# Attention and two expert layers on one core: a key copy to ScalarE, three multiplications to VectorE, one weight piece behind two query loads

## The chip, the cores and the metric

The kernel runs on one core of one Trainium2 chip. The metric is the device time of one execution in microseconds. A core has five engines with a stream of instructions each: PE (TensorE, matmuls, with PEld for its weight loads), DVE (VectorE), ACT (ScalarE), POOL (GpSimd) and SP (SyncE, which only issues DMAs here). An engine works through its stream in order, and waits on semaphores for the others and for DMAs.

## The reference

Inputs are q, k, v (2 batches, 8 heads, 768 positions, 64 columns) and the weights of two dense layers. Attention of a query goes to the keys within 16 positions and to 24 block keys (the maximum over each block of 32); the layers follow on 1536 tokens of width 512.

```python
k_sum = k.reshape(B, H, nb, block, D).max(axis=3)
v_sum = v.reshape(B, H, nb, block, D).mean(axis=3)
scores_s = scale * einsum('bhsd,bhnd->bhsn', q, k_sum) + log(block)
a = softmax(concat([where(|i - j| < 16, scale * q @ k.T, -1e9), scores_s]))
x = a @ concat([v, v_sum])
h = x @ w_in;   x = (h * sigmoid(1.702 * h)) @ w_out          # 512 -> 2048 -> 512
x = (sigmoid(x @ w_gate) * (x @ w_val)) @ w_out2              # 512 -> 1536 -> 512
```

## The kernel before, in words

Attention is cut into 24 units: batch (2) by group of four blocks of 64 queries (3) by pair of heads (4). Unit u of batch 0 uses the keys k0_(u mod 4); units 0 to 3 are group 0, units 12 to 23 are batch 1. For each unit `w_copy` (L693) makes a scaled copy kx of the keys that its four blocks see: 96 windowed columns a block (128x384) and 32 block keys a block (128x128), on POOL. `b_pe` (L706) computes mask and scores into PSUM (ps_s, L710 and L712), `b_max` (L715) their maximum on DVE, `b_exp` (L720) the exponentials on ACT, with the sums beside them, `n_inv` (L730) the reciprocal sums on DVE, and `n_mul` (L737) multiplies the 128x512 exponentials e by them, on POOL. `c_pe` (L741) transposes e on PE (ps_p, L745), `c_copy` (L748) copies that from PSUM (ACT for the first ten units), `d_pe` (L753) multiplies by the values vwin and the block values vs (ps_x, L764), `d_hi` (L781) and `d_lo` (L784) write the result as high and low part, xH on ACT and xL on DVE.

The units are written out as a software pipeline: in step t the part with lag n works on unit t - n. The list is

```python
ORDER = [
    (w_copy, -1), (b_pe, 0), (b_max, 0), (n_inv, LN), (n_mul, LN),
    (c_pe, LC), (c_copy, LC), (d_pe, LD), (d_hi, LD), (b_exp, 0), (d_lo, LD),
]
```

with LN = 1 and LC = LD = 3. From step 8 on, pieces of the first expert layer are put between the units (a generator, `filler`): hidden products ps_h, a sigmoid on ACT (L524), its product with the hidden value on DVE (L500), a cast of the result into gh on ACT (L508) and its rest gl, and the output products ps_o (L489). Sigmoid and exponential are different table sets of ACT; a load (ACT_TABLE_LOAD) stands in its stream wherever it goes from one to the other. Every product is made of three, because each fp32 operand is split into a high and a low part.

After attention come the rest of layer 1 (eight groups of hidden columns) and layer 2 (six groups), in which PE runs without a hole.

Loads are issued by SP in the order in which the program writes them. `load_q` (L632, 256 KB a unit, five buffers) runs five units ahead, `load_k` (L626) brings 400 KB a head pair, `load_v` (L642) 768 KB a group, `put_v` (L650) lays the block values of 256 KB beside them, the first time through ACT's queue. `fetch` (L229) issues the next megabyte of weights from a list: first group 0's w_in (`raw1_0_0`), then group 0's w_out, whose name is 1_0_1 and which goes into a buffer with the tag xH, then group 1's. In step 0, `fetch` is called behind the loads of the second group's values, and the load of q6 stands in step 1.

SP's stream is the order of the program. The order of PE, DVE, ACT and POOL is set by the framework's scheduler, which lists the instructions by its own estimate of when each can start; where durations or dependencies change, the order changes with them.

Of the kernel before, what the change touches and what calls it, by code (L numbers as in the profile page):

```python
# [13 lines left out]
AF = mybir.ActivationFunctionType  # L14
ALU = mybir.AluOpType
AX = mybir.AxisListType
PSUM = bass.MemoryType.PSUM
P = 128
# [11 lines left out]
def attention_moe_moe2_kernel(ctx: ExitStack, tc: tile.TileContext, ins: dict, out: bass.AP):  # L30
    nc = tc.nc
# [4 lines left out]
    B, HP, _, S = vt.shape  # L36
# [8 lines left out]
    G = 4  # L45
# [7 lines left out]
    scale = 1.0 / float(D) ** 0.5  # L53
# [169 lines left out]
    for layer, g, i in wanted:  # L223
        w = mats[layer][i]
        last = i == len(mats[layer]) - 1
        x = w.bitcast(U32)
        pieces.append((f"{layer}_{g}_{i}", rows_of(x, g) if last else cols_of(x, g, 2)))

    def fetch():  # L229

        if pieces:
            name, src = pieces.pop(0)
            n, m = src.shape[1], src.shape[2]

            home, tag = (xp, "xH") if name == "1_0_1" else (wraw, "raw")
            raw = home.tile([P, n * m], U32, tag=tag, name=f"{tag}{name}")
            nc.sync.dma_start(out=raw.rearrange("p (a n) -> p a n", a=n), in_=src)
            raws.append((raw, (P, n, m // 2)))
# [357 lines left out]
    def pull(n):  # L596
        for _ in range(n):
            next(coming, None)
# [9 lines left out]
    with tc.manual_schedule(engines={mybir.EngineType.SP}), ExitStack() as es:  # L608
# [17 lines left out]
        def load_k(b, hp):  # L626

            t = kp.tile([P, SH], F32, tag="k", name=f"k{b}_{hp}")
            nc.sync.dma_start(out=t, in_=k[b, hp])
            kraw[b, hp] = t  # L630

        def load_q(u, eng):  # L632

            b, g, hp = units[u]
            t = qp.tile([P, G, P], F32, tag="q", name=f"q{u}")
            eng.dma_start(out=t.rearrange("p i c -> p (i c)"), in_=q[b, g, hp])
            qbd[u] = t
# [4 lines left out]
        def load_v(b, g):  # L642
            c = (b * NG + g) % 2 * G
            first_row = v[b, g * G * QB:g * G * QB + P - W0, :]
            src = bass.AP(
                first_row.tensor, first_row.offset, [first_row.ap[0], [QB * H * D, G], [1, H * D]]
            )
            nc.sync.dma_start(out=vwin[W0:P, c:c + G, :], in_=src)

        def put_v(b, g, eng=nc.sync):  # L650
            c = (b * NG + g) % 2 * G
            src = vsum[b][0:W0].unsqueeze(1).to_broadcast([W0, G, H * D])
            eng.dma_start(out=vwin[0:W0, c:c + G, :], in_=src)
# [5 lines left out]
        def sum_load(b, hp):  # L659
            if (b, hp) == (0, 2):  # L660
                early = xp.tile([P, 2, KC * TB // 2], F32, tag="xL", name="vt_early")
                vtl["early"] = [early[:, i, 0:S] for i in range(2)]
            if b == 0 and hp > 1:
                t = vtl["early"][hp - 2]
            else:
                t = vp.tile([P, S], F32, tag="vt", bufs=2, name=f"vt{b}_{hp}")
            nc.sync.dma_start(out=t, in_=vt[b, hp])
            vtl[b, hp] = t

        def sum_v(b, hp):  # L670
            if hp == 0:
                vpart[b] = vp.tile([P, HP, W0], F32, tag="vm", name=f"vm{b}")
                nc.vector.memset(vpart[b], 0.0)
            nc.vector.tensor_reduce(
                out=vpart[b][:, hp, 0:NB], in_=vtl.pop((b, hp)).rearrange("p (n t) -> p n t", t=BLK),
                axis=AX.X, op=ALU.add,
            )

        def sum_lay(b):
            r = vpart.pop(b)  # L680
            ps = ps_a.tile([W0, H * D], F32, tag="x", name="ps_v", bufs=2)
            for hp in range(HP):
                nc.tensor.matmul(ps[:, hp * P:(hp + 1) * P], lhsT=r[:, hp], rhs=ident, start=True, stop=True)
            nc.scalar.activation(vsum[b][0:W0], ps, AF.Copy, scale=1.0 / BLK)

        def prep_k(b, hp):
            ks = kp.tile([P, W0], F32, tag="ks", name=f"ks{b}_{hp}")
            nc.vector.memset(ks, 0.0)
            own = kraw[b, hp][:, HALO:HALO + S].rearrange("p (n t) -> p n t", t=BLK)
            nc.vector.tensor_reduce(out=ks[:, 0:NB], in_=own, axis=AX.X, op=ALU.max)  # L690
            kmax[b, hp] = ks

        def w_copy(u):  # L693

            b, g, hp = units[u]
            t = kxp.tile([P, G, P], F32, tag="kx", name=f"kx{u}")
            r = kraw[b, hp][:, g * G * QB:g * G * QB + P - W0]
            src = bass.AP(r.tensor, r.offset, [r.ap[0], [QB, G], [1, P - W0]])
            top = kmax[b, hp].unsqueeze(1).to_broadcast([P, G, W0])
            for to, x in ((t[:, :, W0:P], src), (t[:, :, 0:W0], top)):  # L700
                nc.gpsimd.tensor_scalar(out=to, in0=x, scalar1=scale, scalar2=None, op0=ALU.mult)  # L701
            kx[u] = t

# [32 lines left out]

        def n_mul(u):  # L737
            e, rr = live["e", u], live.pop(("rr", u))
            nc.gpsimd.tensor_tensor(out=e, in0=e, in1=rr.unsqueeze(2).to_broadcast([P, G, P]), op=ALU.mult)

        def c_pe(u):  # L741
            e = live.pop(("e", u))
# [41 lines left out]
        def d_lo(u):  # L784
# [5 lines left out]
        LN, LC, LD = 1, 3, 3  # L790
# [4 lines that stand above are left out]
# [6 lines left out]
        for _ in range(4):  # L801
# [28 lines left out]
            out=win, in_=win, pattern=[[0, NSLOT], [1, P - W0]], compare_op=ALU.is_gt, fill=NEG,  # L830
# [3 lines left out]
            out=win, in_=win, pattern=[[0, NSLOT], [-1, P - W0]], compare_op=ALU.is_gt, fill=NEG,  # L834
# [21 lines left out]
        for t in range(-1, NU + LD):  # L856
            now[0] = t

            u = t + 2
            if u < NU and units[u][1] == 0:  # L860
                prep_k(units[u][0], units[u][2])
            for part, lag in ORDER:
                if 0 <= t - lag < NU:
                    part(t - lag)
            if 0 <= t < NU - 5:
                load_q(t + 5, nc.sync)
            if t == -1:
                sum_v(0, 0)
                sum_v(0, 1)
            if t == 0:  # L870
                sum_v(0, 2)
                sum_v(0, 3)
                sum_lay(0)
                load_v(0, 1)
                put_v(0, 1, nc.scalar)
                fetch()
            if t in (5, 8):
                fetch()
            if t in (7, 8, 9, 10):
                sum_load(1, t - 7)  # L880
            if t in (8, 9, 10, 11):
                sum_v(1, t - 8)
            if t == 11:
                sum_lay(1)

            if t % HP == HP - 1 and HP < t < NU - HP:
                c = t // HP + 1
                load_v(c // NG, c % NG)
                put_v(c // NG, c % NG)
            if 8 <= t < 8 + HP:  # L890
                load_k(1, t - 8)
            if t >= 1:
                pull(1 if t < 6 or t > 9 else 2)
            for _ in range(2 if t >= 8 else 1):
                next(fill, None)
# [164 lines left out]
```

## Time and profile before

| | before |
|---|---|
| three runs, us | 615.36, 615.39, 616.43 (median 615.39) |
| the profiled execution, us | 616.76 |
| its span, us | 615.0 |
| its mean granted clock of TensorE | 0.994 |
| instructions | 8762 |

The rows that follow below come from the profiled execution, with times in microseconds from the start of its span. The span is from the first to the last instruction; the 1.76 us between it and the execution's time lie around it.

### The profile page before, as it was taken

What the parts mean: (1) busy time and instruction counts of PE and PEld (TensorE: products, weight loads), DVE (VectorE), ACT (ScalarE), POOL (GpSimd) and SP (SyncE); (2) the same over time, 40 slices, a digit from 0 to 9 for tenths busy, and PEclk for the clock granted to TensorE, in tenths of its full rate; (3) what the DMA queues carried; (4) which work ended last, traced back from release to release, by engine and by line L of the source; (5) the groups of instructions that cost most, each with busy time, mean ns of one, the idle gap of its engine ahead of it and who ended that gap; (6) DMA issues with size and microseconds to landing.
All of it is one profiled execution on the core that took longest, in us unless ns stands there. A gap on an engine that the chain in (4) does not pass through costs nothing.

```text
span 615.0 us, 8762 instructions
## 1 busy us (share of the span) xinstructions
PE 600.4 (98%) x3342; PEld 500.6 (81%) x3342; DVE 447.2 (73%) x668; ACT 316.5 (51%) x624; POOL 188.0 (31%) x158
## 2 busy tenths in 40 slices
PE   7698999999999999999999999999999999999997
PEld 4587788788888888888888888898898898898896
DVE  6599775498998757777559889568759669777434
ACT  4779566666464535535435667635445246344230
POOL 5887586300142413313322021022022022122030
PEclk9989999999999999999999999999999999999999
DMA  9999653003142302321002023322222212200014
GB/s 307 340 277 340 225 147 69 2 10 129 48 148 78 102 36 79 115 81 58 12 1 69 0 68 100 107 69 70 68 69 69 68 69 70 69 1 0 1 51 154
DMA packets 25161, 58.10 MB, mean 94 GB/s; under 512 B 1568, under 2 KB 1824, under 8 KB 25120
## 3 DMA queue, kind: packets, MB, share of 16 engines
q1 hardware_dynamic: 24400, 56.24, 28.0%
q10 hardware_dynamic: 720, 1.31, 0.6%
q8 instruction: 26, 0.43, 0.3%
q14 instruction: 15, 0.12, 0.1%
HBM read 53.08 MB, written 3.15 MB: 91 GB/s over the span
## 4 chain that ended last, share of the span: by engine, by line
PE 93%; DMA 4%; ACT 1%; DVE 1%; POOL 0%; issue 0%; SPq 0%; POOLq 0%
PE ps_o L489 37%; PE ps_y L197 16%; PE ps_x L197 11%; PE ps_v L197 11%; PE ps_h L489 6%; PE ps_h L197 4%; PE ps_s L712 3%; DMA q<-in_q 3%; PE ps_x L764 2%; PE ps_p L745 2%; DMA k<-in_k 1%; PE ps_s L710 0%; ACT L524 0%; ACT e L725 0%; POOL kx L701 0%
## 5 line engine op out<-in xcount | busy, mean ns | idle before, releaser
L511 POOL TENSOR_TENSOR gl<-sg,gh 128x512 fp32r<-128x512 f32 x78 | 114.0, 1467 | 388.6 <-ACT gh L508 246.3
L577 DVE TENSOR_TENSOR acc<-ps_o,acc 128x512 f32<-128x512 f32 x143 | 96.6, 685 | 58.0 <-PE ps_o L489 57.7
L489 PE MATMUL ps_o<-gl,w_1H 128*128 128x512 f32 x192 | 75.4, 394 | 0.0
L489 PE MATMUL ps_o<-gh,w_1H 128*128 128x512 f32 x192 | 74.7, 390 | 0.0
L489 PE MATMUL ps_o<-gh,w_1L 128*128 128x512 f32 x192 | 71.9, 398 | 1.7 <-ACT gh L508 1.7
L508 ACT CAST gh<-sg 128x512 fp32r<-128x512 f32 x84 | 51.6, 621 | 32.8 <-DVE sg L500 24.9
L489 PE MATMUL ps_o<-w_2L,gh 128*128 128x512 f32 (+1 forms) x146 | 56.6, 387 | 0.0
L489 PE MATMUL ps_o<-w_2H,gh 128*128 128x512 f32 (+1 forms) x146 | 56.4, 386 | 0.0
L489 PE MATMUL ps_o<-w_2H,gl 128*128 128x512 f32 (+1 forms) x146 | 56.2, 389 | 0.1
L150 DVE SCALAR_TENSOR_TENSOR da<-da,db 128x1024 uint32<-128x1024 uint32 x34 | 45.7, 1343 | 8.8 <-ACT da L140 8.2
L489 PEld LDWEIGHTS ps_o<-gh,w_1L 128*128 128x128 f32 x192 | 36.1, 189 | 9.2 <-ACT gh L508 1.9
L140 ACT ACTIVATE da<-da 128x1024 f32<-128x1024 f32 x34 | 36.1, 1061 | 13.9 <-DVE da L132 10.7
L489 PEld LDWEIGHTS ps_o<-gl,w_1H 128*128 128x128 f32 x192 | 36.2, 189 | 7.3 <-issue 0.2
L489 PEld LDWEIGHTS ps_o<-gh,w_1H 128*128 128x128 f32 x192 | 36.2, 188 | 7.3
L701 POOL TENSOR_SCALAR kx<-k 128x384 f32<-128x384 f32 x24 | 33.5, 1396 | 18.2 <-PE ps_s L712 10.3
L725 ACT ACTIVATE e<-ps_s,nm 128x128 f32<-128x128 f32 x96 | 34.2, 376 | 9.3 <-DVE nm L717 7.1
L712 PE MATMUL ps_s<-kx,q 128*128 128x128 f32 x192 | 30.9, 314 | 3.3 <-DMA q<-in_q 2.4
L712 PEld LDWEIGHTS ps_s<-kx,q 128*128 128x128 f32 x192 | 28.2, 222 | 6.4 <-DMA q<-in_q 2.3
L489 PEld LDWEIGHTS ps_o<-w_2H,gh 128*128 128x128 f32 x146 | 27.4, 188 | 5.7
L489 PEld LDWEIGHTS ps_o<-w_2H,gl 128*128 128x128 f32 x146 | 27.4, 188 | 5.2 <-DVE acc L577 0.3
L489 PEld LDWEIGHTS ps_o<-w_2L,gh 128*128 128x128 f32 x146 | 27.5, 188 | 5.0
L132 DVE TENSOR_SCALAR db<-raw 128x1024 uint32<-128x1024 uint32 x33 | 28.1, 850 | 0.4
(245 smaller groups left out, 1495.7 us busy)
## 6 DMA issues: line engine op xcount, KB each, us to landing
raw<-in_moe_w_out SPq DMA_DIRECT2D x13, 1024.0 KB, 5.0
raw<-in_moe_w_in SPq DMA_DIRECT2D x8, 1024.0 KB, 7.3
raw<-in_moe_w_gate SPq DMA_DIRECT2D x6, 1024.0 KB, 5.1
raw<-in_moe_w_val SPq DMA_DIRECT2D x6, 1024.0 KB, 5.0
q<-in_q SPq DMA_DIRECT2D x20, 256.0 KB, 9.0
vwin<-in_v SPq DMA_DIRECT2D x6, 768.0 KB, 7.9
k<-in_k SPq DMA_DIRECT2D x8, 400.0 KB, 8.1
out<-acc SPq DMA_DIRECT2D x11, 256.0 KB, 2.0
```

The source lines that it names most:

```text
L132: ins = nc.vector.tensor_scalar(**x)
L140: nc.scalar.activation(af, af, AF.Prelu, scale=REBIAS, alpha=-2.0 ** 32)
L150: ins = nc.vector.scalar_tensor_tensor(out=a, in0=a, scalar=3, in1=b, op0=ALU.logical_shift_left, op1=ALU.bitwise_or)
L197: nc.tensor.matmul(ps, lhsT=a[x][:, kk, :], rhs=b[y][:, kk, :], start=start and i == 0, stop=i == n - 1, skip_group_check=True,)
L489: nc.tensor.matmul(ps, lhsT=a, rhs=b, start=i == 0, stop=i == n - 1)
L508: nc.scalar.copy(gh, sg)
L511: engine.tensor_tensor(out=gl, in0=sg, in1=gh, op=ALU.subtract)
L577: added[layer, g, blk, m] = nc.vector.tensor_tensor(out=a[:, m, :], in0=ps, in1=a[:, m, :], op=ALU.add)
L701: nc.gpsimd.tensor_scalar(out=to, in0=x, scalar1=scale, scalar2=None, op0=ALU.mult)
L712: nc.tensor.matmul(ps[:, j, :], lhsT=t[:, j, :], rhs=kt[:, j, :], start=False, stop=j == G - 1)
L725: nc.scalar.activation(e[:, j, :], s[:, j, :], AF.Exp, bias=nm[:, j:j + 1], accum_out=sm[:, j:j + 1])
L745: nc.tensor.transpose(ps[:, j, :], e[:, j, :], ident)
```

## The change

Three edits. Unit 3's two key copies (u == HP - 1, HP being 4) go by ScalarE's activation with the scale instead of POOL. The multiplication of the exponentials by their reciprocal sums goes by VectorE for units 0 to 2. And the call that fetches group 0's output weights moves from step 0 to step 2, in which it stands behind the loads of q6 and q7.

```diff
@@ w_copy
             for to, x in ((t[:, :, W0:P], src), (t[:, :, 0:W0], top)):
+                if u == HP - 1:
+                    nc.scalar.activation(to, x, AF.Copy, scale=scale)
+                    continue
                 nc.gpsimd.tensor_scalar(out=to, in0=x, scalar1=scale, scalar2=None, op0=ALU.mult)
@@ n_mul
-            nc.gpsimd.tensor_tensor(out=e, in0=e, in1=rr.unsqueeze(2).to_broadcast([P, G, P]), op=ALU.mult)
+            (nc.vector if u < HP - 1 else nc.gpsimd).tensor_tensor(out=e, in0=e, in1=rr.unsqueeze(2).to_broadcast([P, G, P]), op=ALU.mult)
@@ the steps
                 put_v(0, 1, nc.scalar)
-                fetch()
-            if t in (5, 8):
+            if t in (2, 5, 8):
                 fetch()
```

Three lines more stand ahead of what follows, so a line of the kernel before has a number higher by 3 in the changed one from L701 on, and by 2 behind the steps.

SP's queue, at the place of the moved fetch. A row is the line, the kind of instruction, and what goes into what, with the buffers' numbers. Before:

```order
L237 DMA raw1_0_0_152<-in_moe_w_in 128x4x512
L636 DMA q5_209<-in_q 128x512
L648 DMA vwin_109<-in_v 96x4x512
L237 DMA xH1_0_1_221<-in_moe_w_out 128x2x1024
L636 DMA q6_248<-in_q 128x512
L636 DMA q7_278<-in_q 128x512
L636 DMA q8_331<-in_q 128x512
```

And of the change:

```order
L237 DMA raw1_0_0_152<-in_moe_w_in 128x4x512
L636 DMA q5_209<-in_q 128x512
L648 DMA vwin_109<-in_v 96x4x512
L636 DMA q6_246<-in_q 128x512
L636 DMA q7_276<-in_q 128x512
L237 DMA xH1_0_1_278<-in_moe_w_out 128x2x1024
L636 DMA q8_331<-in_q 128x512
```

The megabyte of weights has gone behind q6 and q7; ahead of q8 stands the same as before.

PE, from the transposes of unit 4 to the scores of unit 8 (ps_p are transposes, ps_s scores and their masks, ps_x the products with the values). Before:

```order
L745 MATMUL ps_p_454<-ident_67,e_325 128x128 x4
...
L712 MATMUL ps_s_441<-kx6_386,q6_248 128x128 x4
L712 MATMUL ps_s_498<-kx7_438,q7_278 128x128 x4
L710 LDWEIGHTS pick_111
L710 MATMUL ps_s_547<-mask_110,pick_111 128x512
...
L745 MATMUL ps_p_511<-ident_67,e_377 128x128 x4
L712 MATMUL ps_s_547<-kx8_495,q8_331 128x128 x4
```

And of the change:

```order
L748 MATMUL ps_p_454<-ident_67,e_325 128x128 x4
L715 MATMUL ps_s_441<-kx6_386,q6_246 128x128 x4
L767 MATMUL ps_x_409<-pt_407,vwin_109 64x64
...
L715 MATMUL ps_s_498<-kx7_438,q7_276 128x128 x4
L748 MATMUL ps_p_511<-ident_67,e_377 128x128 x4
L713 LDWEIGHTS pick_111
L713 MATMUL ps_s_547<-mask_110,pick_111 128x512
L715 MATMUL ps_s_547<-kx8_495,q8_331 128x128 x4
```

Unit 6's scores now stand ahead of the value products, and unit 7's behind them; unit 8's scores close the piece in both.

ScalarE, around the second step's two sigmoids (sg, from the hidden products ps_h) and the exponentials e of units 14 and 15. Before:

```order
L782 CAST xH1_765<-ps_x_956 128x256
L725 ACTIVATE e_967,sm_966<-ps_s_936,nm_942 128x128 x4
L573 COPY acc1_0_853<-ps_o_918 128x512
L573 COPY acc1_0_853<-ps_o_926 128x512
L524 ACT_TABLE_LOAD
L524 ACTIVATE sg_1049<-ps_h_978 128x512
L508 CAST gh1_1_0_0_1054<-sg_1049 128x512
L524 ACTIVATE sg_1051<-ps_h_991 128x512
L508 CAST gh1_1_0_1_1059<-sg_1051 128x512
L782 CAST xH1_765<-ps_x_1027 128x256
L725 ACT_TABLE_LOAD
L725 ACTIVATE e_1038,sm_1037<-ps_s_1007,nm_1013 128x128 x4
```

And of the change:

```order
L524 ACT_TABLE_LOAD
L524 ACTIVATE sg_1049<-ps_h_978 128x512
L508 CAST gh1_1_0_0_1054<-sg_1049 128x512
L785 CAST xH1_765<-ps_x_956 128x256
L728 ACT_TABLE_LOAD
L728 ACTIVATE e_967,sm_966<-ps_s_936,nm_942 128x128 x4
L524 ACT_TABLE_LOAD
L524 ACTIVATE sg_1051<-ps_h_991 128x512
L508 CAST gh1_1_0_1_1059<-sg_1051 128x512
L785 CAST xH1_765<-ps_x_1027 128x256
L785 CAST xH1_765<-ps_x_1086 128x256
L728 ACT_TABLE_LOAD
```

The exponentials e_967 have come between the two sigmoids, with a table load on either side.

## Rows read from the trace of the kernel before

**Rows 1.** The page, busy time, share of the span and instructions of each engine.
```profile
PE 600.4 (98%) x3342; PEld 500.6 (81%) x3342; DVE 447.2 (73%) x668; ACT 316.5 (51%) x624; POOL 188.0 (31%) x158
```

**Rows 2.** Windows: start:end, length, busy us (instructions) by engine, PE clock, DMA share, GB/s.
```profile
15.00:30.00 15.00, 10.60 (x143) 8.18 (x143) 8.65 (x20) 11.13 (x42) 13.30 (x14) 1.00 1.05 337
30.00:45.00 15.00, 14.02 (x132) 11.99 (x132) 13.81 (x29) 10.36 (x38) 11.96 (x11) 0.89 0.92 273
45.00:60.00 15.00, 13.22 (x127) 10.28 (x126) 14.07 (x24) 13.94 (x39) 11.19 (x11) 0.95 1.04 372
75.00:500.00 425.00, 424.98 (x2211) 355.32 (x2210) 319.88 (x445) 224.02 (x392) 110.84 (x85) 1.00 0.22 72
```

**Rows 3.** The chain of waits in order of time: start us, us, what.
```profile
15.92 14.98 DMA q<-in_q
```

**Rows 4.** DMA issues at 11.2 (vwin), 13.1, 15.9 and 19.55: KB, us to landing.
```profile
vwin<-in_v SPq DMA_DIRECT2D x1, 768.0 KB, 14.2
xH<-in_moe_w_out SPq DMA_DIRECT2D x1, 1024.0 KB, 17.3
q<-in_q SPq DMA_DIRECT2D x1, 256.0 KB, 15.0
q<-in_q SPq DMA_DIRECT2D x1, 256.0 KB, 12.7
```

**Rows 5.** PE's timeline: start, us, line, operation, [idle before <-releaser]; units 6+7, 8, 12.
```profile
30.95 3.63 PE L712 MATMUL ps_s<-kx,q 128*128 128x128 f32 x16 [2.19 <-DMA q<-in_q]
...
36.40 1.06 PE L712 MATMUL ps_s<-kx,q 128*128 128x128 f32 x8
...
53.90 1.05 PE L712 MATMUL ps_s<-kx,q 128*128 128x128 f32 x8
...
58.21 0.61 PE L489 MATMUL ps_o<-gh,w_1L 128*128 128x512 f32 x1 [1.72 <-ACT gh L508]
```

**Rows 6.** POOL's timeline: unit 3's key copy, and unit 12's.
```profile
13.27 1.17 POOL L701 TENSOR_SCALAR kx<-k 128x384 f32<-128x384 f32 x1 [1.41 <-DMA k<-in_k]
...
49.55 1.39 POOL L701 TENSOR_SCALAR kx<-k 128x384 f32<-128x384 f32 x1 [1.37 <-DMA k<-in_k]
```

**Rows 7.** The page's groups: VectorE's accumulation; busy us, mean ns, idle before it.
```profile
L577 DVE TENSOR_TENSOR acc<-ps_o,acc 128x512 f32<-128x512 f32 x143 | 96.6, 685 | 58.0 <-PE ps_o L489 57.7
```

**Rows 8.** VectorE's timeline, its two long waits between 16 and 21 us.
```profile
16.62 0.95 DVE L674 TENSOR_REDUCE vm<-vt_early 128x24 f32<-128x768 f32 x1 [0.93 <-DMA vt_early<-in_vt]
...
20.46 1.29 DVE L717 TENSOR_REDUCE nm<-ps_s 128x4 f32<-128x512 f32 x2 [1.82 <-PE ps_s L712]
```

**Rows 9.** ScalarE's timeline: unit 1's exponentials, table loads, casts and a sigmoid's wait.
```profile
12.87 0.37 ACT L725 ACTIVATE e<-ps_s,nm 128x128 f32<-128x128 f32 x1 [1.32 <-DVE nm L717]
...
58.17 1.28 ACT L725 ACT_TABLE_LOAD   x1
59.47 0.37 ACT L725 ACTIVATE e<-ps_s,nm 128x128 f32<-128x128 f32 x1
...
60.85 0.63 ACT L508 CAST gh<-sg 128x512 fp32r<-128x512 f32 x1
...
73.78 1.28 ACT L524 ACT_TABLE_LOAD   x1 [2.85 <-PE ps_h L489]
...
76.43 0.62 ACT L508 CAST gh<-sg 128x512 fp32r<-128x512 f32 x1 [0.76 <-DVE sg L500]
```

**Rows 10.** Windows as in rows 2: the two falls of the clock, and between them 3 us.
```profile
31.50:33.00 1.50, 1.50 (x9) 1.50 (x9) 1.50 (x4) 0.00 (x0) 0.00 (x0) 0.50 1.05 382
34.50:37.50 3.00, 3.00 (x47) 2.44 (x45) 2.88 (x6) 2.33 (x12) 3.00 (x3) 0.99 0.56 171
58.50:60.00 1.50, 1.50 (x8) 1.40 (x8) 1.50 (x2) 1.49 (x4) 1.20 (x2) 0.50 1.03 233
```

## The prediction, made before the changed kernel had run

> **What bounds the kernel now.** I read the page first: TensorE is busy 98% of the span, the others 73, 51 and 31% [rows 1]. Its time can therefore only change through its few holes or its clock, and the windows say where these are: PE is busy 10.60 of 15 us from 15 to 30, and 424.98 of 425 us from 75 to 500 [rows 2]. Attention's first half is the only place where this change can win anything, and what it wins there comes off the end, because PE then has no hole left to swallow it.
>
> Next the chain of waits: one transfer of queries, from 15.92 for 14.98 us, is its longest piece, and the scores of units 6 and 7 begin when it lands [rows 3, 5]. The queue view shows why the transfer takes so long: group 0's output weights (1024 KB) are issued at 13.1 and q6 behind them at 15.9. They land 17.3 and 15.0 us later, at 30.4 and 30.9, and q8, issued at 19.55, lands 12.7 us later, at 32.25 [rows 4]. These are not slow transfers: the DMA engines are busy throughout (share 1.05) and move 337 GB/s from 15 to 30 [rows 2]. It is a backlog, in which a transfer's place decides its landing and its issue time does not.
>
> PE's own timeline then gives the dates that matter: units 6 and 7 at 30.95 after a hole of 2.19 us, unit 8 at 36.40, unit 12 at 53.90, and the first output product at 58.21 after a hole of 1.72 us behind ScalarE's cast [rows 5].
>
> **The change part by part.** *Early copies and multiplications.* POOL loses unit 3's key copy, 1.17 us and a smaller one [rows 6], and three multiplications. VectorE gains the three. None of this form ran on it; its nearest row of 128x512 elements is the accumulation at 685 ns [rows 7], so 3 x 0.685 = 2.06 us. They fall where VectorE waits: 0.93 us for a value transfer and 1.82 us for scores [rows 8], 2.75 us together. ScalarE gains two copies. Its cast of 512 columns takes 0.63 us [rows 9], so I put at most that for 384 columns and as much for 128. Unit 3's keys are there only when POOL starts on them at 13.27 after waiting 1.41 us [rows 6], and in the new order ScalarE does the first of these copies ahead of unit 1's exponentials, which began at 12.87 [rows 9]: they move to 13.27 + 0.63 = 13.90, about 1 us later. Whether this group gains or loses that microsecond, its successors wait for queries until past 30 us, so I cost it at nothing. If the queries came early enough, unit 1's delay would be the price: the bounds are 1 us lost, and 1.70 us gained (POOL's copies).
>
> *The queries' place.* Between the values issued at 11.2, which land 14.2 us later at 25.4 [rows 4], and q6 the megabyte of weights no longer stands. Then 256 KB at 337 GB/s take 0.8 us: q6 lands at about 26.2 and q7 at 27.0; with ScalarE's 256 KB value-sum transfer sharing the engines in that stretch it may be a microsecond more. Unit 6 no longer waits. But q8 and all behind it have the same bytes ahead as before and keep 32.25. In the new order PE does units 6 and 7 and the older products, comes to unit 8's scores, and waits there for q8. So unit 8 goes from 36.40 to 32.25: **4.15 us is the ceiling**, not the 30.95 - 26.2 that the move of q6 suggests. PE's work between is 36.40 - 30.95 = 5.45 us and fits behind 27.0.
>
> *What of the lead reaches the end.* From 36.40 to 45 PE has hardly a hole (14.02 us of 30 to 45 are busy, and most of the rest is the end of the hole at 30.95 [rows 2, 5]), so the lead lasts that long. Unit 12 needs the second batch's keys, for which POOL waited 1.37 us at 49.55 [rows 6]. They can come earlier only as far as the DMA engines have room. From 34.5 to 37.5 they moved 171 GB/s against 382 from 31.5 to 33.0 [rows 10]: 3 x (382 - 171) = 633 KB are missing there, which is 1.7 us at that rate. The first output product at 58.21 hangs on ScalarE, which is busy 13.94 of the 15 us from 45 to 60 [rows 2] and can start only as early as its inputs. So the lead there lies between 1.7 and 4.15. I take 2.5 us, nearer the keys, because those are the row with a wait in it.
>
> *Table loads.* The new order of ScalarE has two more table loads, as unit 14's exponentials now stand between the two sigmoids of the second step. Each costs 1.28 us [rows 9]. In that stretch ScalarE idled 2.85 us ahead of the sigmoid at 73.78 and 0.76 us ahead of its cast at 76.43 [rows 9]. The second sigmoid now comes behind load, exponentials (59.47 to 60.85 for unit 12's four, 1.38 us) and load, 1.28 + 1.38 + 1.28 = 3.94 us. Less 2.85 us that leaves 1.09, less 0.76 us as well 0.33. I take 0.6 us lost; the bounds are 0, since PE may have other work there, and the whole 3.94.
>
> *The clock.* Two stretches ran at half clock (granted 0.50, 1.2 of 2.4 GHz): one around 31.5 to 33.0, behind the 2.19 us hole, and one around 58.5 to 60.0, behind the 1.72 us hole [rows 5, 10]. Unit 6's and 7's sixteen score matmuls took 3.63 us there, unit 8's eight 1.06 us at full clock [rows 5]: 3.63 - 2 x 1.06 = 1.5 us is what the first cost at least. The first is inside the 4.15 already: its loss only delayed unit 8, which the new date of q8 replaces. If the hole ahead of unit 8 is as deep, the fall moves there and costs up to 1.5 us of the lead. The second stays if its hole stays: I take 0, with the same 1.5 us of gain as the other bound.
>
> *Sum:* 0 - 2.5 + 0.6 + 0 = **-1.9 us**. The profiled execution took 616.76 us (span 615.0), 1.37 us over the median of 615.39. Taken from the median: **613.5 us**.
>
> **The rivals.** *A, the whole lead arrives:* unit 12's keys had slack, and 4.15 us reach the end, or the second fall of the clock goes as well. For it: POOL has the first part of the copy done at 49.55 + 1.39 = 50.94, while the scores that need it come at 53.90 [rows 5, 6]. Against it: the copy waited for them at all. 615.39 - 4.15 = 611.2; with the second clock fall gone and 0.6 lost to the tables 610.3.
>
> *B, the lead is eaten:* keys and ScalarE's row of work stand where they stood, and by 58.21 nothing is left but the hole ahead of that product, now longer. For it: ScalarE has 1.06 us of slack in those 15 us, and it is its cast that ended PE's hole at 58.21 [rows 2, 5]. The same comes out if the queue does not serve in the order of issue and q6 is early in the program only. Time: 615.39 with 0.6 for the tables, 615.0 to 616.
>
> *C, slower:* PE stalls for the second sigmoid. The price is the whole 3.94 us on PE's path, against a lead of 2.5: +1.4, so 616.8. It decides from the point at which PE has no other product ready while ScalarE loads. For it: from 75 on PE has no hole that could swallow a wait [rows 2], and its order is fixed. Against it: ScalarE had its 2.85 us of idle time precisely there. The rule that would make this dearer is in the Trainium skill, "ScalarE: Activation LUTs", section "What ACT_TABLE_LOAD costs": a switch costs the load and a drain of about the same length, some 2.66 us together. By that two more would be an estimated 5.3 us. The trace differs: the load at 58.17 took 1.28 us and the exponential behind it began at 59.47, 1.30 us after the load's start [rows 9], so the measured price holds here.
>
> **How the numbers follow.** A measurement of this kernel can tell 0.2%, or 1.2 us, from no change. Forecast (611.9 to 614.4): 0.40. A: 0.17, since a wait for keys stands in the rows. B: 0.24, since ScalarE is nearly full where the lead has to pass. C: 0.19, since ScalarE's idle covers most of its price. Faster: 0.40 + 0.17 = 0.57; the same 0.24; slower 0.19. The range reaches from between the two times of A, at 610.8, to just over C, 617.0. The forecast's own range is 611.9 (a lead of 4.15 with no clock gain and 0.6 for the tables) to 614.4 (a lead of 1.7 and 0.7 lost).
>
> **What would show it.** Right: q6 lands before 28 and q8 still near 32; PE's hole of 2.19 us is ahead of unit 8 and no longer ahead of unit 6; unit 8 starts near 32.3; the first output product starts 1.7 to 4 us ahead of 58.21; between two sigmoids of the second step stand two table loads, and PE's wait behind them is under 1 us. Wrong: unit 8 starts later than 34; or the first output product is at 58 still, which is B; or PE has a hole of more than 1 us between 70 and 80, which is C. A median under 610.8 would mean that both clock falls are gone and the keys never mattered.

## The result, and the profile after

The changed kernel took **618.50 us** (median of 7 executions, 617.04 to 619.65) against 615.36 for the kernel before (7 executions, 614.20 to 616.43): slower by half a per cent, ratio 1.0052, 95% interval 1.0041 to 1.0062. Forecast were 613.5 and a range up to 617.0: the prediction was wrong in sign and in range. The profiled execution of the changed kernel took 617.66, with a span of 615.9.

The page of the changed kernel, its line of busy times, which answers to [rows 1]:

```profile
PE 600.7 (98%) x3341; PEld 500.2 (81%) x3342; DVE 451.1 (73%) x671; ACT 319.7 (52%) x628; POOL 184.4 (30%) x153
```

Its windows, with the columns of [rows 2], show where PE's holes went. From 15 to 30 it is now busy 13.76 us, against 10.60. From 70 on, where it had none, there are holes: 2.52 us between 70 and 90 and half a microsecond between 90 and 110.

```profile
15.00:30.00 15.00, 13.76 (x197) 11.40 (x195) 13.05 (x26) 12.81 (x51) 13.25 (x13) 1.00 1.05 337
45.00:60.00 15.00, 13.47 (x96) 10.00 (x91) 15.00 (x23) 10.11 (x27) 12.00 (x10) 0.89 1.00 343
70.00:90.00 20.00, 17.48 (x131) 13.76 (x133) 12.41 (x26) 13.11 (x43) 13.88 (x15) 1.00 0.86 260
90.00:110.00 20.00, 19.51 (x174) 15.86 (x175) 11.40 (x25) 13.01 (x48) 14.23 (x15) 1.00 0.28 67
```

The queue did what the forecast said. SP's timeline has q6 issued at 12.37 and q8 at 17.36:

```profile
12.37 3.59 SPq L636 DMA_DIRECT2D q<-in_q  x2
...
17.36 2.81 SPq L636 DMA_DIRECT2D q<-in_q  x2
```

and the DMA issues at 12.4 and at 17.4 show q6 landing 13.0 us later at 25.4 (30.9 before [rows 4]) and q8 14.0 later at 31.4 (32.25 before):

```profile
q<-in_q SPq DMA_DIRECT2D x1, 256.0 KB, 13.0
q<-in_q SPq DMA_DIRECT2D x1, 256.0 KB, 14.0
```

PE's timeline: unit 6 follows q6 at 25.40, unit 8 waits for q8 until 31.46, as forecast, with a hole of only 1.10 us and no fall of the clock behind it. At 52.41 PE waits for ScalarE's copy of a transpose, and at 56.05 it starts the first output product (58.21 before). The last four rows are the 2.52 us between 70 and 90: a wait for a score buffer that unit 14's exponentials give back (74.96), one for VectorE's copy of a transpose (76.02), one for the second step's second gated value (sg, multiplied by VectorE right behind ScalarE's sigmoid, 77.60), and one for a score buffer that unit 15's exponentials give back (85.16). Only 0.30 us of them is a wait for the second sigmoid.

```profile
25.40 1.16 PE L715 MATMUL ps_s<-kx,q 128*128 128x128 f32 x8 [0.25 <-DMA q<-in_q]
...
31.46 1.13 PE L715 MATMUL ps_s<-kx,q 128*128 128x128 f32 x8 [1.10 <-DMA q<-in_q]
...
52.41 0.97 PE L748 MATMUL ps_p<-ident,e 128*128 128x128 f32 x4 [1.53 <-ACT pt L753]
...
56.05 0.73 PE L489 MATMUL ps_o<-gh,w_1L 128*128 128x512 f32 x2
...
74.96 0.38 PE L713 MATMUL ps_s<-mask,pick 128*128 128x512 bf16 x1 [0.66 <-ACT e L728]
...
76.02 0.69 PE L767 MATMUL ps_x<-pt,vwin 128*64 128x64 f32 x16 [0.69 <-DVE pt L753]
...
77.60 0.50 PE L489 MATMUL ps_o<-gh,w_1L 128*128 128x512 f32 x1 [0.30 <-DVE sg L500]
...
85.16 0.38 PE L713 MATMUL ps_s<-mask,pick 128*128 128x512 bf16 x1 [0.87 <-ACT e L728]
```

ScalarE's timeline from 68 on is the row of work that stands behind these waits: table load, sigmoid, cast, load, unit 14's four exponentials, load, the second sigmoid, its cast. It has 1.11 us of idle time ahead of it and 0.76 twice, each time for its own product on VectorE. Then a cast waits 3.45 us for PE, with the next table load and unit 15's exponentials queued behind it. These exponentials begin at 83.6; before, they began at 80.5.

```profile
68.55 1.28 ACT L524 ACT_TABLE_LOAD   x1 [1.11 <-PE ps_h L489]
69.85 0.60 ACT L524 ACTIVATE sg<-ps_h 128x512 f32<-128x512 f32 x1
71.20 0.62 ACT L508 CAST gh<-sg 128x512 fp32r<-128x512 f32 x1 [0.76 <-DVE sg L500]
...
72.11 1.28 ACT L728 ACT_TABLE_LOAD   x1
73.41 0.37 ACT L728 ACTIVATE e<-ps_s,nm 128x128 f32<-128x128 f32 x1
...
74.93 1.28 ACT L524 ACT_TABLE_LOAD   x1
76.22 0.60 ACT L524 ACTIVATE sg<-ps_h 128x512 f32<-128x512 f32 x1
77.58 0.62 ACT L508 CAST gh<-sg 128x512 fp32r<-128x512 f32 x1 [0.76 <-DVE sg L500]
...
81.92 0.37 ACT L785 CAST xH<-ps_x 128x256 fp32r<-128x256 f32 x1 [3.45 <-PE ps_x L767]
82.31 1.28 ACT L728 ACT_TABLE_LOAD   x1
```

### The profile page after: what moved, and what is told of

Its sections match the earlier page's. It is cut to its first block, busy times and chain, and to the rows that moved or that the text cites. A ratio compares the mean times of both kernels' runs of the same rounds, so it can differ in the third digit from the quotient of the medians.

```text
span 615.9 us, 8755 instructions
## 1 busy us (share of the span) xinstructions
PE 600.7 (98%) x3341; PEld 500.2 (81%) x3342; DVE 451.1 (73%) x671; ACT 319.7 (52%) x628; POOL 184.4 (30%) x153
## 4 chain that ended last, share of the span: by engine, by line
PE 87%; ACT 5%; DMA 5%; DVE 2%; issue 0%; ACTq 0%; SPq 0%
PE ps_o L489 37%; PE ps_y L197 16%; PE ps_x L197 11%; PE ps_v L197 11%; PE ps_h L489 5%; PE ps_h L197 4%; DMA xH<-in_moe_w_out 2%; ACT e L728 2%; DMA vt_early<-in_vt 1%; PE ps_x L767 1%; PE ps_s L715 1%; DMA q<-in_q 1%; PE ps_p L748 1%; ACT L728 1%; ACT L524 1%; ACT sg L524 1%
## 5 line engine op out<-in xcount | busy, mean ns | idle before, releaser
L489 PE MATMUL ps_o<-gh,w_1H 128*128 128x512 f32 x192 | 74.7, 390 | 0.0
L508 ACT CAST gh<-sg 128x512 fp32r<-128x512 f32 x84 | 51.4, 620 | 32.8 <-DVE sg L500 24.9
L704 POOL TENSOR_SCALAR kx<-k 128x384 f32<-128x384 f32 x23 | 28.6, 1245 | 11.6 <-PE ps_s L715 8.1
```

The source lines that it names most:

```text
L489: nc.tensor.matmul(ps, lhsT=a, rhs=b, start=i == 0, stop=i == n - 1)
L508: nc.scalar.copy(gh, sg)
```

## The experiments

The theories. **T:** the two extra table loads in the second step cost the time. **T2:** not the loads as such but the place of sigmoids and exponentials in ScalarE's stream. **K:** the early edits themselves (the key copy, the multiplications, the keys) make it slower. **S:** SP's queue stands still ahead of the second batch's last keys. **B:** a lead made early is eaten by what comes next. **L:** a lead survives if ScalarE is in order. **F:** the end is set behind attention. **R:** the first profile of the kernel before was not a typical execution. Each set of runs has its own executions of the kernel before beside it; ratios are to these. A profile shows one execution of a run, which can be its fastest or its slowest.

**A second profile of each of the two kernels** (no edit).

The kernel before:

> The kernel before, unchanged, another execution in the profile. Theory R (the profiled execution of before, 616.76, 1.4 us over its median, had one more half-clock stretch than most): one of the two stretches, around 31 to 34 or 58 to 62, is missing, and the work done by 90 us is 1 to 1.7 us ahead of the first profile's. Rival: both are there again, and the difference of 1.4 us lies elsewhere.

The changed kernel:

> The changed kernel, unchanged, another execution. Theory T2: PE is again held up between 70 and 86 us behind the second step's second sigmoid, by over 2.5 us against the kernel before. Rival: that stretch was a chance of the first profile, and the loss lies elsewhere this time.

They took 615.72 and 618.15. Starts in PE's timelines, in us:

| | before, first | before, again | changed, first | changed, again |
|---|---|---|---|---|
| scores of unit 8 | 36.40 | 34.20 | 31.46 | 32.07 |
| scores of unit 11 | 46.39 | 45.72 | 40.54 | 41.01 |
| scores of unit 12 | 53.90 | 53.23 | 53.17 | 53.53 |
| scores of unit 16 | 78.30 | 77.06 | 80.11 | 80.54 |
| scores of unit 20 | 94.36 | 93.33 | 96.94 | 97.38 |
| first hidden product of the fourth step | 114.05 | 113.01 | 114.98 | 115.43 |
| the execution | 616.76 | 615.72 | 617.66 | 618.15 |

Between the two second profiles the difference is 2.42 us at the fourth step and 2.43 at the end: nothing happens behind attention. The lead of 4.7 us at unit 11 is gone at unit 12, where the changed kernel is 0.3 behind.

A unit's start is not all of PE's work, though, because the two orders put different work between the units. An estimate of the whole comes from adding up the matmuls that PE has begun, each weighted with the usual time to the next where PE is full (0.227 us for one of 512 columns, 0.112 for a block of scores). One score mask has no record in the changed kernel's traces and is counted in. By this estimate the changed kernel (again) is 2.4 us ahead of the kernel before (again) at 45 us, level at 54, 1.2 ahead at 72, 2.0 behind at 90, and 2.4 behind at the end. So most of the loss is made between 72 and 90 us, and it is 3.1 us there (3.1 as well from the first profile of the changed kernel).

Theory R holds, though its stretches are others than it named. The windows of the second profile of the kernel before:

```profile
15.00:30.00 15.00, 11.62 (x136) 9.19 (x135) 10.10 (x21) 9.62 (x36) 11.52 (x13) 0.89 1.05 341
45.00:60.00 15.00, 13.22 (x129) 10.45 (x125) 14.07 (x25) 13.94 (x39) 11.79 (x11) 1.00 0.98 332
70.00:90.00 20.00, 20.00 (x151) 16.22 (x149) 15.41 (x34) 11.71 (x41) 16.68 (x18) 1.00 0.61 201
```

It has one stretch at half clock (1.2 of 2.4 GHz), between 18 and 22 us, while the backlog of transfers lasts. The two at 31 and 58 are both missing. PE's timeline has no wait for q6 at all, and the hole ahead of the first output product is the same 1.72 us, without a fall of the clock:

```profile
30.38 2.05 PE L712 MATMUL ps_s<-kx,q 128*128 128x128 f32 x16
...
57.54 0.50 PE L489 MATMUL ps_o<-gh,w_1L 128*128 128x512 f32 x1 [1.72 <-ACT gh L508]
```

Theory T2's place is confirmed. The windows of the second profile of the changed kernel have the same holes from 70 on, 2.53 and 0.47 us, while its clock was full from 15 to 110:

```profile
70.00:90.00 20.00, 17.47 (x142) 13.66 (x139) 12.03 (x25) 13.56 (x44) 13.89 (x15) 1.00 0.87 263
90.00:110.00 20.00, 19.53 (x170) 16.03 (x169) 11.61 (x27) 12.57 (x45) 14.13 (x15) 1.00 0.28 67
```

With 0.10 us from 60 to 70 PE's holes from 60 to 110 are 3.10 us, in the kernel before (again) 0.71: a difference of 2.39. That it equals the 2.43 at the end is in part chance: by the estimate above the changed kernel is still ahead at 72, and its four holes from there to 90 cost more than the 2.5 us that PE stands idle in them.

What moved is unit 14's exponentials. In the second profile of the kernel before they stand ahead of the step's sigmoids; in the changed kernel they begin at 73.41, behind the first sigmoid and a load. That is 6.5 us later, though the unit's scores come only 3.4 us later (68.31 against 64.91):

```profile
66.91 0.37 ACT L725 ACTIVATE e<-ps_s,nm 128x128 f32<-128x128 f32 x1 [0.23 <-DVE nm L717]
```

**The second step's order mended.**

```diff
@@ sigmoid, in first()
+    exps, after_exp = {}, {(1, 0): 14}
-            nc.scalar.activation(sg, ps, AF.Sigmoid, scale=1.702)
+            ins = nc.scalar.activation(sg, ps, AF.Sigmoid, scale=1.702)
+            if batch and (g, blk) in after_exp:
+                behind(ins, exps[after_exp[g, blk]])
@@ b_exp
-                nc.scalar.activation(
+                exps[u] = nc.scalar.activation(
```

> The changed kernel, with the second step's sigmoids ordered behind unit 14's exponentials, so that the two extra table loads between the two sigmoids go and PE's order stays as it is in the changed kernel. Theory T (the extra loads on ScalarE cost the time): in the changed kernel's trace PE idles 0.76 us from 60 to 75 and 1.86 us from 75 to 90, and nothing there before; that goes to under 0.5 us in 60 to 90, and the median falls by about 3 us from 618.5 to about 615.5 (614.5 to 616.3). Rival K (the early edits or the keys of the second batch make it slower): the median stays within 1 us of 618.5.

616.29 (615.24 to 617.96), ratio 1.0014 (1.0005 to 1.0023). Of the loss of 0.52% this edge of order on ScalarE gives back 0.38, and K falls. But PE's order did not stay, as the expectation took for granted: the scheduler listed PE's stream anew with the edge, and from 72.85 us on it differs (score masks and output products of the second step). So the run shows that the order in this step is what costs; it does not part ScalarE's order from PE's. About 0.9 us of loss is left by the ratio, and PE still has 1.54 us of holes from 70 to 90 in the profiled execution, which is the fastest of the eleven (615.24). The chain of waits of this run names the rest, from the block values' sums on ScalarE over SP's queue and the last keys to VectorE and PE's products (1.48 us of waiting at 74.71, for the cast that stands behind VectorE's work):

```profile
66.46 0.41 ACT vs L688
...
66.89 0.61 SPq L657
...
67.59 4.20 DMA k<-in_k
...
71.81 0.95 DVE ks L694
...
74.71 0.50 PE ps_o L489
```

**The last keys ahead in SP's queue,** in addition:

```diff
-            if t % HP == HP - 1 and HP < t < NU - HP:
-                c = t // HP + 1
-                load_v(c // NG, c % NG)
-                put_v(c // NG, c % NG)
             if 8 <= t < 8 + HP:
                 load_k(1, t - 8)
+            if t % HP == HP - 1 and HP < t < NU - HP:
+                c = t // HP + 1
+                load_v(c // NG, c % NG)
+                put_v(c // NG, c % NG)
```

> The changed kernel with the sigmoids ordered as in the first experiment, and in SP's queue the second batch's last keys (k1_3) moved ahead of the block values that SP waits for ScalarE to write. Theory S (what is left of the loss, and the lead, are held up at SP: k1_3 was issued at 67.6 behind that wait, VectorE waited for it, and PE for VectorE): k1_3 lands before 66, PE's hole of 1.48 us at 74.7 goes, and the median falls from 616.29 to about 614.8 (614.0 to 615.4). Rival B (something else takes the lead): within 0.5 us of 616.3.

615.05 against 615.17 (ratio 1.0004, 0.9995 to 1.0012). In the profiled execution, the fastest of its eleven (614.50), the hole at 74.7 is gone, and PE is busy 19.42 of the 20 us. The median moved as S said. The intervals of this run and the one before overlap, so the 0.6 us between them is likely and not certain. With both, the loss is gone, and there is still no gain.

**The edits alone and in pairs.** Queries alone (the moved fetch):

> Only the fetch of group 0's output weights moves behind q6 and q7; copies and multiplications stay on POOL. ScalarE's order keeps its number of table loads. Theory T: the lead of the queries (about 4 us at unit 8) is kept in part, 613.5 (612 to 615). Rival K: the moved fetch itself harms (later weights, keys), so that it is slower than 615.4 by over 1 us. Rival B (a lead made early is eaten by what comes next): 614.8 to 616.

615.29 against 615.51, ratio 1.0000 (0.9992 to 1.0009): B. Queries and multiplications:

> The fetch moved and the multiplications of units 0 to 2 on VectorE, unit 3's key copy left on POOL. The number of table loads stays that of before. Theory T: no loss, as the queries alone or better, 613 to 615. Rival K: VectorE's three multiplications delay its successors, 616.5 or more.

615.52, ratio 1.0003 (0.9994 to 1.0011): no loss, no gain. Queries and key copy:

> The fetch moved and unit 3's key copy on ScalarE, the multiplications left on POOL. ScalarE's order has the same two extra loads between the second step's sigmoids as the changed kernel. Theory T: as slow as the changed kernel, 618.5 (617.5 to 619.5), with PE holes from 70 to 90. Rival K: if the multiplications on VectorE were what costs, about 615.

618.79, ratio 1.0055 (1.0040 to 1.0070), with 3.21 us of holes from 70 to 90: the same loss at the same place, without the multiplications. Key copy alone:

> Only unit 3's key copy on ScalarE; multiplications on POOL, fetch where it was. Two extra table loads stand around the third step's second sigmoid, none in the second step. Theory T2 (not the number of loads but the second step's second sigmoid coming behind unit 14's exponentials costs, where PE has run ahead): 615.2 (614.5 to 616), since the second step's order is that of before. Rival K (the key copy on ScalarE itself, which delays unit 1's exponentials by a microsecond): 617 or more.

617.86 against 615.32, ratio 1.0045 (1.0031 to 1.0058): T2 missed this one. The second step is in order here (19.92 busy from 70 to 90), but its third step, with the extra loads, loses 1.93 us in the profiled execution, the fastest of the five (616.47):

```profile
90.00:110.00 20.00, 18.07 (x155) 14.64 (x157) 9.02 (x23) 16.01 (x47) 10.62 (x12) 1.00 0.25 54
```

Key copy and multiplications:

> Key copy and multiplications moved, fetch where it was. Extra loads in the third step only. Theory T2: 615.2 (614.5 to 616). Rival K: 617 or more.

615.19, ratio 1.0000 (0.9991 to 1.0009). The same extra loads stand in the third step, with 1.07 us of holes from 90 to 110, and a lead made earlier balances them: unit 18's scores start at 81.71, against 83.85 in the second profile of the kernel before. So the key copy as such is not what costs. Multiplications alone:

> Only the multiplications of units 0 to 2 on VectorE. ScalarE's order has two extra table loads as well, but between the sigmoids of the third step, around unit 18's exponentials. Theory T: these cost there too, 617 to 618.5. Rival K: the loads cost only where PE has run ahead, 615.4.

614.90 against 615.17, ratio 1.0006 (0.9994 to 1.0018), with 0.72 us of holes from 90 to 110. T, that two loads cost 2.6 us wherever they stand, falls.

**Two loads and nothing else,** in the kernel with queries and multiplications:

```diff
-            held = [(ps, sigmoid(ps)) for ps in held]
+            if (g, blk) == (1, 0):
+                one, two = held
+                held = [(one, sigmoid(one))]
+                between = nc.scalar.activation(dummy, ident[:, 0:1], AF.Exp)
+                behind(between, sig[-1])
+                held.append((two, sigmoid(two)))
+                behind(sig[-1], between)
+            else:
+                held = [(ps, sigmoid(ps)) for ps in held]
```

> The queries moved and the multiplications on VectorE (which measured as before, 615.52), with one exponential of a single column put between the second step's two sigmoids, so that ScalarE loads its tables twice more there: two loads and one tiny operation, and nothing else moved on PE. Theory T: slower by 2.6 us (the two loads, 2 x 1.28) or a little more, 617.5 to 618.8, with a hole of PE ahead of the products that need the second cast. Rival K: no change, 615.5.

615.85 against 615.17, ratio 1.0010 (1.0001 to 1.0019), where it was 1.0003 (0.9994 to 1.0011) without them: the intervals overlap, so the price of the two loads, 0.07%, is not told apart from nothing. PE's order is the same with them as without. ScalarE's timeline has the two loads, and the second cast at 78.87, later than in the changed kernel (77.58):

```profile
74.08 1.28 ACT L537 ACT_TABLE_LOAD   x1
75.37 0.20 ACT L537 ACTIVATE dummy<-ident 128x1 f32<-128x1 f32 x1
...
76.22 1.28 ACT L526 ACT_TABLE_LOAD   x1
...
78.87 0.62 ACT L508 CAST gh<-sg 128x512 fp32r<-128x512 f32 x1 [0.50 <-DVE sg L500]
```

Still PE is busy 19.99 of 20 us from 70 to 90. Here PE has other work in its stream ahead of the product that needs this cast. In the changed kernel, the exponentials of unit 14 and what hangs on them are late as well: PE's waits at 74.96, 76.02 and 85.16.

**Other orders.** Queries and multiplications, with the last keys ahead as above:

> The queries moved and the multiplications on VectorE (615.52), and k1_3 ahead of the block values in SP's queue. Theory S: 614 to 615. Rival B: 615.5, because the third late input (ScalarE's full row of work ahead of the first output product) holds it.

617.42, ratio 1.0041 (1.0029 to 1.0053): slower, a miss of S. PE is busy 20.00 us from 70 to 90 and loses 1.05 from 90 to 110, and 0.6 more than without the edit from 60 to 70. The move of one load changed the third step's order again. One number (EARLY_UNITS from 10 to 8) in the changed kernel, and in the kernel before:

> The changed kernel with one number changed: the transposes of units 8 and 9 are copied from PSUM by VectorE instead of ScalarE. ScalarE's order then has no extra table loads, and its row of work ahead of the first output product is shorter by two copies of 0.6 us; PE's hole of 1.53 us at 52.4, which ended with ScalarE's copy, should go with the fall of the clock behind it. Theory T2 with B (ScalarE holds the lead up at two places, 50 to 58 and 70 to 86): 613.5 (612.5 to 614.8). Rival K: 617 or more. Rival F (the end is set by something behind attention whatever comes earlier): 615 to 616.

> The kernel before with the same number changed and nothing else. Theory B: PE's hole of 1.72 us at 58.2 behind ScalarE's cast shrinks, 614 (613 to 615). Rival F: 615.2.

615.46 (ratio 1.0001, 0.9992 to 1.0010) and 617.28 (1.0030, 1.0018 to 1.0041). An edit that has nothing to do with the change takes its whole loss away, and costs the kernel before two microseconds (2.05 us of holes from 60 to 70). The forecast gain of B came in neither. In the first of them PE's wait for ScalarE's copy ahead of unit 12 is gone, and unit 12 starts no earlier, because PE now waits there for the key copy on POOL:

```profile
53.82 1.43 PE L715 MATMUL ps_s<-kx,q 128*128 128x128 f32 x5 [1.71 <-POOL kx L704]
```

**The third step's order mended,** without the moved fetch, with the diff of the first experiment and the entry (0, 1): 20. Multiplications alone:

> The multiplications of units 0 to 2 on VectorE alone (614.9 against 615.17, with a lead of over 3 us until 95 us in its profile, of which 2 go around the two extra loads of the third step), and that step's sigmoids ordered behind unit 20's exponentials, which takes the extra loads away. Theory L (the lead survives once nothing on ScalarE stands in its way): 613.5 (612.8 to 614.5). Rival F: 615.

Key copy and multiplications:

> Key copy and multiplications moved, fetch where it was (615.19), with the same order in the third step. Theory L: 613.8 (613 to 614.8). Rival F: 615.2.

614.45 (ratio 0.9993, 0.9981 to 1.0005) and **614.34** against 615.43 (ratio 0.9987, 0.9978 to 0.9995). The second is the one version faster than the kernel before clear of its interval, by about 0.8 us by the ratio. Its median lies in L's range, and the gain is about half of what L forecast. It is one of sixteen edited versions and was measured in one set, so it is likely and not certain.

**All three edits with both orders,** with entries (1, 0): 14 and (0, 1): 20, and the same with the last keys ahead:

> All three edits, with the sigmoids of the second and of the third step ordered behind the exponentials of units 14 and 20. Theory B (the lead of the queries is gone at unit 12, which waits for the second batch's keys and ScalarE, whatever comes earlier): not faster than without the moved fetch, 615 to 616.3. Rival L (the lead is worth its forecast once ScalarE is mended): 613 to 614.

> The same, with the second batch's last keys ahead of the block values in SP's queue. Theory B: 614.3 to 615.3, as without the moved fetch at best. Rival L: 612.5 to 613.8.

620.12 (ratio 1.0091, 1.0069 to 1.0112) and 621.20 (1.0092, 1.0077 to 1.0108), the slowest of all, though ScalarE has no more table loads than in the kernel before. ScalarE's timeline of the first of them, third step: the edge holds the sigmoids back to 103.44, and the scheduler then put both casts behind one more load and the next exponentials.

```profile
102.14 1.28 ACT L526 ACT_TABLE_LOAD   x1
103.44 1.09 ACT L526 ACTIVATE sg<-ps_h 128x512 f32<-128x512 f32 x2
...
107.48 1.14 ACT L508 CAST gh<-sg 128x512 fp32r<-128x512 f32 x2
```

PE's timeline has the waits, and in this execution the clock fell behind them (0.85 granted from 110 to 125). It is the slowest of the six, at 623.02; the two whose granted clock was 1.000 took 619.01 and 619.05, so some 4 us of the loss need no fall of the clock:

```profile
106.34 0.69 PE L771 MATMUL ps_x<-pt,vwin 128*64 128x64 f32 x16 [1.58 <-DVE pt L757]
...
108.16 1.22 PE L489 MATMUL ps_o<-gh,w_1L 128*128 128x512 f32 x2 [0.55 <-ACT gh L508]
```

That is the plainest case for T2: the number of loads is that of before, their place is not. As in the first experiment, PE's order changed with the edge.

## Why the prediction was wrong, point by point

*Early edits, cost nothing:* right as to their direct cost: together, without the moved fetch, they measured 1.0000. What they cost indirectly is the order behind 60 us; the key copy alone measured 0.45% slower, with its holes behind 60 us mostly in the third step. And they do more than nothing early: with the multiplications alone unit 11 starts at 42.68, with the moved fetch alone at 44.53, in the second profile of the kernel before at 45.72. By these single profiles more of the lead comes from the early edits than from the queries.

*The queries' place:* right. q6 at 25.4 (26.2 forecast), q8 at 31.4 (32.25), unit 8 at 31.46 and 32.07 (32.25). But the ceiling of 4.15 us was taken from one execution. In the second profile unit 8 started at 34.20 in the kernel before, which leaves 2.1 us of lead there. The 2.19 us hole and the fall of the clock at 31 belonged to that first execution, and so they should not have been carried over to the median.

*What of the lead reaches the end, 1.7 to 4.15, taken 2.5:* **this step failed first.** Unit 12's scores start at 53.17 and 53.53 in the changed kernel, 53.23 in the second profile of the one before: nothing arrives there, and in all profiles but the last two of the experiments unit 12 starts between 51.4 and 53.9, wherever between 40.1 and 46.4 unit 11 started. The 633 KB that the DMA engines could make up existed in full in the first execution only (in the second they moved 361 GB/s from 34.5 to 36.0 and 253 from 36.0 to 37.5). POOL's timelines show the keys and then their block maxima (the rows name rr, VectorE's reciprocal, which ends 0.1 us behind the block maxima ks). In the changed kernel:

```profile
49.26 1.17 POOL L704 TENSOR_SCALAR kx<-k 128x384 f32<-128x384 f32 x1 [0.47 <-DMA k<-in_k]
51.21 1.50 POOL L704 TENSOR_SCALAR kx<-ks 128x128 f32<-128x128 f32 x1 [0.78 <-DVE rr L737]
```

and in the second profile of the kernel before:

```profile
48.56 1.71 POOL L701 TENSOR_SCALAR kx<-k 128x384 f32<-128x384 f32 x1 [1.05 <-DMA k<-in_k]
52.09 0.53 POOL L701 TENSOR_SCALAR kx<-ks 128x128 f32<-128x128 f32 x1 [1.82 <-DVE rr L734]
```

Both have the copy whole at 52.6 to 52.7 (53.44 in the second profile of the changed kernel). The keys stand behind the same bytes in the queue either way. In the changed kernel ScalarE's copy, for which PE waits at 52.41, ends at nearly the same time, so unit 12 has two limits there; with that copy moved to VectorE the wait for the key copy on POOL holds it at 53.82. That is rival B as far as unit 12. It is not B at the first output product, which B had at 58 still: that starts at 56.05 and 55.25, against 58.21 and 57.54, where the kernel before waits 1.72 us for ScalarE's cast. So a lead of about 1.2 us (the estimate above, at 72) came through, where 2.5 were taken. The moved fetch alone (1.0000) agrees with B, but it is no test of it: in its profile the lead at unit 11 is only 1.2 us.

*Table loads, 0.6 lost:* **this step failed second, and by more.** The place was right, the second step's two sigmoids with unit 14's exponentials between them, and so was the chain of load, exponentials and load ahead of the second sigmoid. The size was not: from 60 to 110 PE's holes are 2.4 us more than in the kernel before, and by the estimate above the second step cost 3.1 us, against the 0.6 taken and the bound of 3.94. I had subtracted ScalarE's 2.85 us of idle time. That idle time was ScalarE waiting for PE's hidden products; these came 4 to 5 us earlier, the idle time shrank to 1.11 (68.55), and unit 15's exponentials, behind a cast that waits for PE, came 3.1 us later. I had also looked at the second sigmoid alone, for which PE waits 0.30 us. The exponentials of unit 14 went behind the first sigmoid and a load, from 66.91 to 73.41, and the other waits hang on exponentials. And the price isn't that of the loads: two loads alone cost 0.07%, not told apart from nothing, in another order of PE. The Trainium skill, "ScalarE: Activation LUTs", section "What ACT_TABLE_LOAD costs", would have made them dearer still, by a drain. Here the load at 74.93 is followed by the sigmoid at 76.22, 1.29 us after its start, so the measured 1.28 stands. With the sizes of the estimate the prediction's sum reads 0 - 1.2 + 3.1 = +1.9 us; the rest of the 2.4 between the two second profiles comes behind 90 us, where PE has one more hole of 0.47 us at 105.

*The clock:* the half-clock stretches came and went between executions (18 to 22, or 31 and 58, or 52.5 to 56 in the changed kernel, or none before 110 us in its second profile), so they explain none of the difference between the two second profiles. They do bear on the medians, which lie 3.1 us apart and not 2.4. The two executions of the changed kernel with a granted clock of 1.000 took 617.04 and 617.52, the five with 0.997 (one such stretch, as in its first profile) 617.66 to 619.65; for the kernel before, over the experiments, 23 with 1.000 have a mean of 614.78 and 65 with 0.997 one of 615.34. A stretch goes with some 1.4 us in the changed kernel and 0.6 in the one before.

*The rivals:* C named the place and nearly the price, with 3.94 less a lead of 2.5, which is 616.8; its stall for the second sigmoid was the smallest of the four waits. B named what happened to the lead at unit 12. Taken as alternatives, each was milder than the two together: C's price without a lead gives up to 615.39 + 3.94 = 619.3, and the range ended at 617.0.

*The signs:* each sign of being right came in the first profile: q6 before 28 and q8 near 32, the hole ahead of unit 8, unit 8 near 32.3, the first output product 2.2 us ahead of 58.21, two loads between the sigmoids and under 1 us of wait behind them. The sign for C did not, as no hole between 70 and 80 is over 1 us: there are three, of 0.66, 0.69 and 0.30, and a fourth at 85. The signs asked for single waits where the sum of the holes over the whole step was needed.

## What to carry to other kernels

Where a scheduler sets the order of in-order engines, an edit at the start can cost its time 50 us later; compare the order of every engine over the whole stretch that moved, and price the new order with the waits as they will be, not with idle time that an engine has only because another one is late. Rivals on one path add up: price the case in which the lead is lost and the new wait is there as well. And profile the kernel before more than once: a hole and a clock fall seen in one execution are not the median's to win.

## What was not expected of the hardware

Executions of one and the same kernel put their waits and their half-clock stretches at quite different places: the kernel before had two, at 31 and 58 us, in one profile and one at 18 to 22 in the other, and units 6 and 7 waited 2.19 us for their queries in the first and not at all in the second. The two executions took 616.76 and 615.72.
